# Decoding float64 weights in halves through PSUM between the products of a mixture of experts

## The chip, the cores and the metric

The kernel runs on one core of a Trainium2 chip. The metric is the device time of one execution in microseconds, the median over several runs. The core's engines are called as the profile calls them: PE (TensorE, matrix products; PEld are its weight loads), DVE (VectorE), ACT (ScalarE), POOL (GpSimd) and SP (SyncE, which issues DMAs).

## The reference

Three layers run one after the other on 3072 tokens. A chunked state-space attention gives rows of 256 numbers. A router sends each row to one of eight experts, each two products with a ReLU between. A dense layer of width 2048 follows, whose weights `w_in` and `w_out` arrive as float64.

```python
h = np.maximum(x[mask] @ w1[e], 0.0)          # eight experts, 256 -> 1024 -> 256
out[mask] = gate_w[mask, None] * (h @ w2[e])
...
h = x @ w_in                                  # 256 -> 2048, float64 weights
g = h * np.cos(h)
return (g @ w_out).astype(np.float32)         # 2048 -> 256
```

## The kernel before, in words

The program has three stages. The first (to about 136 us) computes attention and router and scatters each token's row into its expert's list in DRAM. The second (136 to 297 us) works through eight lists, `for e in range(E)`. The third (from 297 us) is the dense layer. The change lies in the second.

**A list.** List 0 has 256 places, lists 1 to 7 have 432. All products are made of pairs: a number is split into a high part of type fp32r and a remainder of the same type, and three matmuls stand for one. For each eighth f of the hidden width PE makes product f into a PSUM tile `ph` (L1235, six matmuls), ACT takes the ReLU's high part `hh` (L1239), DVE the remainder `hl` (L1240, reading `ph` and `hh`). From f = 3 on PE also makes the second product of f - 3 into `py` (L1203), which reads `hh` and `hl`; those of the last three eighths form the list's tail, after the f loop, for each of two halves m. ACT then copies `py` to `yd` (L1197). `ph` comes from the pool `psH` with four buffers, one PSUM bank each; `px` (the transposed rows of the next list, L1049) has two banks and `py` two.

**What goes beside it.** Between products the program's order on each engine is written out by hand: after each f, `side.take(k)` runs k steps of the decode (below), `next(gt[..])` steps of the gates of the next lists (small DVE instructions on `xg`, such as L840, L846, L863, and an exponential on ACT), and `ws.take()` one step of splitting the next list's weights: a copy `h` on ACT (L743) and a subtraction `l` on POOL (L752). After f = 5 PE transposes the next list's rows; ACT and DVE make `xh` and `xl` of them (L1055, L1057), the latter ahead of the last `hl` of the list.

**The decode.** The dense layer's weights come as float64, 16 pieces of 512 columns by 128 partitions, each 32-bit word of a number beside the other. `fetch(q)` loads piece q into one of two buffers `raw` (SP's queue). The generator `decode()` turns a piece into float32 in steps, one step to each `yield`: ACT scales the high words (`tb`, L1086); DVE shifts them (`ta`, L1088), merges the sign bit (L1090) and the top bits of the low word (L1094, or L1101 into `wof`). For the eight pieces of `w_in` ACT then makes the high part `ih` (L1096) and DVE the remainder `il` (L1098). `ta` and `tb` have one SBUF buffer each. Seven steps make a piece of `w_in`, five one of `w_out`, 96 in all. The generator is started at the end of list 0. The table `g.TE` says how many steps follow each product of each list, `g.SD` how many go into a list's tail: `SD[0]` once and `SD[1]` after each half, the latter not in list 7. In list 7 the split of the decoded output weights (`split_out`, L1114 on ACT and L1115 on POOL) goes beside the last decode steps.

**Loads.** All on SP's queue in the program's order: before list 0, the w2 of list 1 and the rows of list 2 (L883); in list 0, after f = 2 a fill of list 3's unused places (L870), after f = 4 the w1 of list 2 (L729) and, behind it, `fetch(0)` and `fetch(1)` (L1068); then the w2 of list 2 (L735) and the rows of list 3. Later pieces are fetched when the decode begins a piece, one ahead.

Of the kernel before, what the change touches and what calls it, by code (L numbers as in the profile page):

```python
# [8 lines left out]
F32 = mybir.dt.float32  # L9
# [11 lines left out]
NT, D, E, F, F2 = 3072, 256, 8, 1024, 2048  # L21
NSTEP = S // 128
SX = 4096
RW = 274
# [614 lines left out]
TWO_PI = 6.283185307179586  # L639
# [3 lines left out]
def tile_attention_moe_moe2(ctx: ExitStack, tc: tile.TileContext, A1, A2, X, BNh, BT, CT, cst_d, emb, tau, w1, w2, w_in, w_out, out):  # L643
    nc = tc.nc
    ET = mybir.EngineType
    g = G_()
# [19 lines left out]
    g.WARM = 12  # L666
    g.LD = "cnfz"
    g.HEAD = "k2 l0 i1 a0 z0 m0 c1 k2 z1 s1 k3 b0 p1 k6 i1 s2 e0 c2 k2 k1 i9 a1 b1 y0 e0 p2 e0 e0 t1 k6 t1 t1 t1 t1"
    g.SD = (1, 1)
    g.FIRST = 6  # L670
    g.GE = "vava"
    g.GW = "va"
# [8 lines left out]
    g.G1 = [(), (6, 3, 2, 2, 1, 0, 0, 0)] + [(3, 1, 2, 1, 1, 0, 0, 0)] * 6  # L681
    g.G2 = (0, 0, 0, 0, 2, 0, 2, 2)

    g.TE = [(0, 0, 0, 0, 0, 0, 0, 0)] + [(2, 1, 1, 1, 1, 1, 1, 1)] * 4 + [(2, 2, 2, 2, 2, 2, 1, 2)] + [(2, 2, 2, 2, 2, 2, 2, 2)] * 2
    g.L2 = "vvvv"
    g.WL = 16
    g.S1 = ("vvvv", "vpvp")
# [344 lines left out]
    with ExitStack() as mctx:  # L1032
        mp = mctx.enter_context(tc.tile_pool(name="mp", bufs=1, reuse_waits="tile"))
        mp2 = mctx.enter_context(tc.tile_pool(name="mp2", bufs=2, reuse_waits="tile"))
        wpool[1] = mctx.enter_context(tc.tile_pool(name="wB", bufs=1, reuse_waits="tile"))
        psX = mctx.enter_context(tc.tile_pool(name="psX", bufs=1, space=PSUM, reuse_waits="tile"))
        psH = mctx.enter_context(tc.tile_pool(name="psH", bufs=4, space=PSUM, reuse_waits="tile"))
        psO = mctx.enter_context(tc.tile_pool(name="psO", bufs=1, space=PSUM, reuse_waits="tile"))
        wof = mp.tile([128, 16 * D], F32, name="wof")

# [16 lines left out]
            nc.vector.tensor_tensor(out=xl, in0=px[:, :, :n], in1=xh.bitcast(F32), op=ALU.subtract)  # L1057
            yield xh, xl

        PL = 512  # L1060

        src = [w_in.bitcast(U32).rearrange("(k p) (q f) -> k q p f", p=128, f=2 * PL),
               w_out.bitcast(U32).rearrange("(q f p) d -> q p f d", p=128, f=2)]
# [1 line left out]
        def fetch(q):  # L1065
            raw = mp.tile([128, PL, 2], U32, tag="raw", name="raw", bufs=2)
            if q < 8:
                nc.sync.dma_start(raw.rearrange("p f w -> p (f w)"), src[0][q // 4, q % 4])  # L1068
            else:
                nc.sync.dma_start(raw.rearrange("p (f d) w -> p f (d w)", f=2), src[1][q - 8])  # L1070
            return raw

        def decode():

            ihf, ilf = ih.rearrange("p k f -> p (k f)"), il.rearrange("p k f -> p (k f)")
            V_ = nc.vector
            for q in range(16):
                raw = raw_.pop(0)
                if 1 <= q < 15:
                    raw_.append(fetch(q + 1))  # L1080
                L, H = raw[:, :, 0], raw[:, :, 1]
                ta = mp.tile([128, PL], U32, tag="ta", name="ta")
                tb = mp.tile([128, PL], U32, tag="tb", name="tb")
                yield

                nc.scalar.activation(tb.bitcast(F32), H.bitcast(F32), AF.Copy, scale=2.0 ** -112)  # L1086
                yield
                V_.tensor_scalar(ta, tb, 3, 0x7fffffff, op0=ALU.logical_shift_left, op1=ALU.bitwise_and)  # L1088
                yield
                V_.scalar_tensor_tensor(out=ta, in0=tb, scalar=0x80000000, in1=ta, op0=ALU.bitwise_and, op1=ALU.bitwise_or)  # L1090
                yield
                if q < 8:
                    s = slice(PL * q, PL * q + PL)
                    V_.scalar_tensor_tensor(out=ta, in0=L, scalar=29, in1=ta, op0=ALU.logical_shift_right, op1=ALU.bitwise_or)  # L1094
                    yield
                    nc.scalar.activation(ihf[:, s], ta.bitcast(F32), AF.Copy, scale=1.0 / TWO_PI)  # L1096
                    yield
                    V_.scalar_tensor_tensor(out=ilf[:, s], in0=ta.bitcast(F32), scalar=1.0 / TWO_PI, in1=ihf[:, s].bitcast(F32), op0=ALU.mult, op1=ALU.subtract)  # L1098
                else:
                    s = slice(PL * (q - 8), PL * (q - 8) + PL)  # L1100
                    V_.scalar_tensor_tensor(out=wof[:, s].bitcast(U32), in0=L, scalar=29, in1=ta, op0=ALU.logical_shift_right, op1=ALU.bitwise_or)  # L1101
                yield

        O = {}

# [16 lines left out]
        def overflow():  # L1122
            with tc.If(T > 0):
                with tc.For_i(0, T, 1) as i:
                    V_ = nc.vector
# [31 lines left out]
                    w2r = w2.rearrange("e f d -> (e f) d")  # L1157
                    nc.sync.dma_start(v1, w1r[bass.ds(r_1, D), :].rearrange("(k p) f -> p k f", p=128))
                    nc.sync.dma_start(v2, w2r[bass.ds(r_2, F), :].rearrange("(f p) d -> p f d", p=128))
                    vx = mp.tile([128, PL], F32, tag="ta", name="vx")[:, :RW]  # L1160
                    nc.sync.dma_start(vx, xs[bass.ds(r_3, 128), :])
                    ix = mp2.tile([128, 1], F32, tag="ix", name="ix")
                    nc.gpsimd.tensor_copy(ix, vx[:, 273:])
# [4 lines left out]
                        pass  # L1168
                    for m in range(2):
                        nc.tensor.transpose(px[:, m, :128], vx[:, 136 * m:136 * m + 128], ident)  # L1170
                    vt = mp.tile([128, PL], F32, tag="tb", name="vt")[:, :D].rearrange("p (m c) -> p m c", m=2)
                    nc.vector.tensor_copy(vt, px[:, :, :128])
                    py = [psO.tile([128, 512], F32, tag=f"py{m}", name="py") for m in range(2)]
                    vh = wof[:, :1024].rearrange("p (f c) -> p f c", f=8)
# [11 lines left out]
        load_w2(1)  # L1186
        xs_ = {1: xg, 2: rows_of(2)}
        numbers(1, xg, mp2, ET.Pool, nc.gpsimd)
        raw_ = []
        x_ = g.x0  # L1190
        gt = [steps["g"], None]

# [24 lines left out]
        for e in range(E):  # L1217
            w = {k: W[e][k].rearrange("p (a b) -> p a b", a=2 if k[1] == "1" else 8) for k in ("h1", "l1", "h2", "l2")}
            xh, xl = x_
            n = wide(e)  # L1220
            ws = Sides()
            if e + 1 < E:
                ws.add(split_w(e + 1))
            else:
                ws.add(split_out())
            py = [psO.tile([128, 512], F32, tag=f"py{m}", name="py") for m in range(2)]
            hs = {}
            for f in range(8):
# [12 lines left out]
                hs[f] = (hh, hl)
                if f >= 3:
                    q = f - 3
                    hh, hl = hs.pop(q)
                    for m in range(2):
                        second(py, m, q, w, hh, hl)
                side.take(g.TE[e][f])
                if f == 0 and 0 < e < E - 2:
                    xs_[e + 2] = rows_of(e + 2)
                if f == 2 and e + 3 < E:  # L1250
                    fill(e + 3)
                for _ in range((g.G1[e] if e else g.G0)[f] if e < E - 1 else 0):
                    next(gt[0])
                if f == 4 and e + 2 < E:
                    gt[1] = gates(xs_[e + 2], mp2, g.GE, e + 2)
                for _ in range((g.G2 if e else g.G20)[f] if e + 2 < E else 0):
                    next(gt[1])
                if f >= 1 or e == E - 1:
                    ws.take()
                if f == 4 and e + 2 < E:  # L1260
                    load_w1(e + 2)
                if (e, f) == (0, 4):
                    raw_ += [fetch(0), fetch(1)]
                if f == (g.PX if e else g.PX0) and e + 1 < E:
                    px = turn(e + 1, xs_.pop(e + 1))
                if f == (g.PX if e else g.PX0) + 1 and e + 1 < E:
                    tp = turned_parts(e + 1, px)
                    next(tp)
                if e == 0 and f == g.XL0:
                    nx = next(tp)  # L1270
            if e + 1 < E:
                x_ = nx
            ws.drain()
            if e + 2 < E:
                next(gt[1])
            gt[0] = gt[1]
# [182 lines left out]
```

## Time and profile before

| what | us |
|---|---|
| median of 3 runs (580.02 to 585.91) | 580.35 |
| the profiled execution, its own time | 577.3 |
| the profiled execution, span from first to last instruction | 575.6 |
| PE busy in the span | 547.3 |
| DVE busy | 443.9 |
| ACT busy | 298.1 |
| POOL busy | 308.9 |

The profile is of one execution. Its busy shares are averages over three unlike stages; what holds in the list stage is read from that stage's stretches. PE's matmuls overlap, so in a busy stretch the start of one matmul to the start of the next is the measure, not the duration of one.

### The profile page before, as it was taken

The numbers are of one execution on the slowest core, as the hardware profiler recorded it, in microseconds if no ns is written. First come the engines' busy times: TensorE is split into PE (matmuls) and PEld (weight loads), VectorE is DVE, ScalarE is ACT, GpSimd is POOL, SyncE is SP. The second block draws the span as 40 slices with busy tenths as digits, with TensorE's granted clock in tenths as the row PEclk, the third lists the DMA queues.
The fourth block names the chain that finished last, engine by engine and source line by source line (L and its number), as shares of the span: only waits on it lengthen the run. The fifth ranks groups of instructions, "written<-read, shape, count | busy, mean of one in ns | idle before, by whom it ended". The sixth has DMA issues, their size and how long they took to land.

```text
span 575.6 us, 11048 instructions
## 1 busy us (share of the span) xinstructions
PE 547.3 (95%) x4000; PEld 497.1 (86%) x4000; DVE 443.9 (77%) x878; ACT 298.1 (52%) x637; POOL 308.9 (54%) x343
## 2 busy tenths in 40 slices
PE   7798999998878999989999999999999999999994
PEld 5587887898868999989988999999999999999994
DVE  6999999866397898898859877766777777676882
ACT  6163543544375567667647546446445445445562
POOL 4323543462265485465636647647646745755763
PEclk9899999999999999999999999999999999999998
DMA  7899895137766556754210000000100100100000
GB/s 213 233 209 226 203 247 170 41 113 216 227 212 216 186 174 183 246 171 158 73 2 2 1 1 11 26 1 2 38 0 1 38 2 1 38 1 10 29 20 19
DMA packets 28993, 57.00 MB, mean 99 GB/s; under 512 B 7216, under 2 KB 16056, under 8 KB 28184
## 3 DMA queue, kind: packets, MB, share of 16 engines
q1 hardware_dynamic: 26184, 47.77, 29.3%
q0 software_dynamic: 2752, 8.51, 4.5%
q8 instruction: 32, 0.52, 0.4%
q14 instruction: 25, 0.20, 0.1%
HBM read 48.50 MB, written 11.07 MB: 103 GB/s over the span
## 4 chain that ended last, share of the span: by engine, by line
PE 56%; DVE 8%; issue 3%; ACT 2%; POOL 1%; POOLq 0%; ACTq 0%; DVEq 0%
PE po L1378 22%; PE pu L1344 22%; PE py L1203 6%; PE ph L1235 5%; DVE hl L1240 2%; DVE ta L1088 1%; POOL gl L1415 1%; DVE ta L1090 1%; DVE xl L1057 1%; DVE lg L840 1%; ACT hh L1239 1%; ACT h L743 1%; DVE ta L1094 1%; DVE xg L863 1%; PE spare L1344 0%
## 5 line engine op out<-in xcount | busy, mean ns | idle before, releaser
L1415 POOL TENSOR_TENSOR gl<-gg,gh 128x512 fp32r<-128x512 f32 (+1 forms) x111 | 125.8, 1139 | 105.0 <-PE pu L1344 59.7
L1405 ACT ACTIVATE cc<-ff,half 128x512 f32<-128x512 f32 (+1 forms) x112 | 74.3, 663 | 128.3 <-DVE ff L1403 128.2
L1401 DVE TENSOR_SCALAR tt<-pu 128x512 f32<-128x512 f32 (+1 forms) x110 | 67.4, 613 | 64.4 <-PE pu L1344 64.2
L1378 PE MATMUL po<-h,gl 128*128 128x256 f32 x384 | 108.2, 282 | 0.0
L1378 PE MATMUL po<-l,gh 128*128 128x256 f32 x384 | 108.2, 282 | 0.0
L1378 PE MATMUL po<-h,gh 128*128 128x256 f32 x382 | 107.6, 282 | 0.0
L752 POOL TENSOR_TENSOR l<-r,h 128x512 fp32r<-128x512 f32 x50 | 68.0, 1373 | 57.9 <-ACT h L743 57.4
L1378 PEld LDWEIGHTS po<-h,gh 128*128 128x128 f32 x382 | 72.3, 189 | 3.6
L1378 PEld LDWEIGHTS po<-l,gh 128*128 128x128 f32 x384 | 72.6, 189 | 3.1
L1378 PEld LDWEIGHTS po<-h,gl 128*128 128x128 f32 x384 | 73.0, 190 | 0.1
L1403 DVE SCALAR_TENSOR_TENSOR ff<-tt,pu 128x512 f32<-128x512 f32 (+1 forms) x110 | 67.0, 609 | 3.8
L1344 PE MATMUL pu<-yh,il 128*128 128x512 f32 (+1 forms) x192 | 68.5, 357 | 0.0
L1344 PE MATMUL pu<-yh,ih 128*128 128x512 f32 (+1 forms) x192 | 68.2, 355 | 0.0
L1344 PE MATMUL pu<-yl,ih 128*128 128x512 f32 (+1 forms) x192 | 68.0, 354 | 0.0
L1411 DVE SCALAR_TENSOR_TENSOR gg<-pu,cc 128x512 f32<-128x512 f32 (+1 forms) x110 | 66.6, 606 | 0.7 <-ACT cc L1405 0.4
L1414 ACT CAST gh<-gg 128x512 fp32r<-128x512 f32 (+1 forms) x112 | 60.8, 543 | 1.1 <-DVE tt L1401 0.5
L1240 DVE SCALAR_TENSOR_TENSOR hl<-ph,hh 128x432 fp32r<-128x432 f32 (+1 forms) x64 | 36.7, 576 | 22.5 <-ACT hh L1239 22.4
L1203 PE MATMUL py<-hl,h 128*128 128x432 f32 (+1 forms) x128 | 45.7, 357 | 4.7 <-DVE hl L1240 4.4
L1203 PE MATMUL py<-hh,h 128*128 128x432 f32 (+1 forms) x128 | 44.9, 351 | 1.9 <-ACT hh L1239 1.9
L1203 PE MATMUL py<-hh,l 128*128 128x432 f32 (+1 forms) x128 | 44.5, 348 | 0.0
L1239 ACT ACTIVATE hh<-ph 128x432 fp32r<-128x432 f32 (+1 forms) x64 | 32.8, 513 | 22.2 <-PE ph L1235 20.2
L1344 PEld LDWEIGHTS pu<-yl,ih 128*128 128x128 f32 x192 | 36.2, 188 | 5.6
(220 smaller groups left out, 1202.2 us busy)
## 6 DMA issues: line engine op xcount, KB each, us to landing
r<-in_w SPq DMA_DIRECT2D x32, 512.0 KB, 5.5
ac<-acd SPq DMA_DIRECT2D x10, 512.0 KB, 6.7
raw<-in_w_in SPq DMA_DIRECT2D x8, 512.0 KB, 4.5
raw<-in_w_out SPq DMA_DIRECT2D x8, 512.0 KB, 3.3
xg<-xs SPq DMA_DIRECT2D x7, 462.4 KB
xs<-zd SPq DMA_DIRECT2D x5, 462.4 KB
XB<-in_X SPq DMA_DIRECT2D x8, 256.0 KB
bt<-in_BT SPq DMA_DIRECT2D x6, 256.0 KB, 9.0
```

The source lines that it names most:

```text
L752: (nc.vector if engines[q] == "v" else nc.gpsimd).tensor_tensor(out=l[:, s], in0=W[e][rn][:, s], in1=h[:, s].bitcast(F32), op=ALU.subtract)
L1203: nc.tensor.matmul(py[m][:, :b_.shape[1]], lhsT=a_[:, q, 128 * m:128 * m + 128], rhs=b_, start=q == 0 and k == 0, stop=q == 7 and k == 2)
L1239: nc.scalar.activation(hh, ph[:, :n], AF.Relu)
L1240: nc.vector.scalar_tensor_tensor(out=hl, in0=ph[:, :n], scalar=0.0, in1=hh.bitcast(F32), op0=ALU.max, op1=ALU.subtract)
L1344: nc.tensor.matmul(PU[u], lhsT=a_[:, c, 128 * f:128 * f + 128], rhs=b_[:, c], start=c == 0 and k == 0, stop=c == 1 and k == 2)
L1378: nc.tensor.matmul(po[:, i], lhsT=a_[:, s], rhs=b_, start=first and per == 1, stop=q == NF - 1 and k == 2 and i == per - 1)
L1401: nc.vector.tensor_scalar(tt, pu, 0.25, MAGIC, op0=ALU.add, op1=ALU.add)
L1403: nc.vector.scalar_tensor_tensor(out=ff, in0=tt, scalar=-MAGIC, in1=pu, op0=ALU.add, op1=ALU.subtract)
L1405: nc.scalar.activation(cc, ff, AF.Sin, bias=half, scale=-TWO_PI)
L1411: nc.vector.scalar_tensor_tensor(out=gg, in0=pu, scalar=TWO_PI, in1=cc, op0=ALU.mult, op1=ALU.mult)
L1414: nc.scalar.copy(gh, gg)
L1415: (nc.vector if u >= len(units) else nc.gpsimd).tensor_tensor(out=gl, in0=gg, in1=gh.bitcast(F32), op=ALU.subtract)
```

## The change

The decode works in halves of 256 columns. Of each half, the scaled high words and the shifted word lie in one PSUM tile of the new pool `psD` (one bank, one buffer); only the word `tu` between the low-word merge and the sign merge lies in SBUF, with two buffers. The order of the two merges is exchanged. `psH` has three buffers in place of four. A half takes six steps for `w_in` and four for `w_out`, 160 in all, and the tables `g.TE` and `g.SD` are raised. The first two raw loads are issued before list 0, directly behind the rows of list 2, in place of after f = 4 of list 0. (In the overflow path two scratch tiles take the tag `tu`.)

```diff
-    g.SD = (1, 1)
+    g.SD = (2, 2)
...
-    g.TE = [(0, 0, 0, 0, 0, 0, 0, 0)] + [(2, 1, 1, 1, 1, 1, 1, 1)] * 4 + [(2, 2, 2, 2, 2, 2, 1, 2)] + [(2, 2, 2, 2, 2, 2, 2, 2)] * 2
+    g.TE = [(0, 0, 0, 0, 0, 0, 0, 0)] + [(3, 2, 2, 2, 2, 2, 2, 2)] * 4 + [(3, 3, 3, 3, 3, 3, 2, 2)] + [(3, 3, 3, 3, 3, 3, 3, 3)] * 2
...
-        psH = mctx.enter_context(tc.tile_pool(name="psH", bufs=4, space=PSUM, reuse_waits="tile"))
+        psH = mctx.enter_context(tc.tile_pool(name="psH", bufs=3, space=PSUM, reuse_waits="tile"))
+        psD = mctx.enter_context(tc.tile_pool(name="psD", bufs=1, space=PSUM, reuse_waits="tile"))
...
-        PL = 512
+        PL, PH = 512, 256
...
-                L, H = raw[:, :, 0], raw[:, :, 1]
-                ta = mp.tile([128, PL], U32, tag="ta", name="ta")
-                tb = mp.tile([128, PL], U32, tag="tb", name="tb")
-                yield
-
-                nc.scalar.activation(tb.bitcast(F32), H.bitcast(F32), AF.Copy, scale=2.0 ** -112)
-                yield
-                V_.tensor_scalar(ta, tb, 3, 0x7fffffff, op0=ALU.logical_shift_left, op1=ALU.bitwise_and)
-                yield
-                V_.scalar_tensor_tensor(out=ta, in0=tb, scalar=0x80000000, in1=ta, op0=ALU.bitwise_and, op1=ALU.bitwise_or)
-                yield
...
+                for h in range(0, PL, PH):
+                    L, H = raw[:, h:h + PH, 0], raw[:, h:h + PH, 1]
+                    tt = psD.tile([128, 2, PH], F32, tag="tb", name="tb")
+                    tb, ta = tt[:, 0], tt[:, 1]
+                    tu = mp.tile([128, RW], U32, tag="tu", name="tu", bufs=2)[:, :PH]
+
+                    nc.scalar.activation(tb, H.bitcast(F32), AF.Copy, scale=2.0 ** -112)
+                    tb, tv = tb.bitcast(U32), ta.bitcast(U32)
                     yield
+                    V_.tensor_scalar(tv, tb, 3, 0x7fffffff, op0=ALU.logical_shift_left, op1=ALU.bitwise_and)
                     yield
+                    V_.scalar_tensor_tensor(out=tu, in0=L, scalar=29, in1=tv, op0=ALU.logical_shift_right, op1=ALU.bitwise_or)
+                    yield
+                    s = slice(PL * (q % 8) + h, PL * (q % 8) + h + PH)
+                    if q < 8:
+                        V_.scalar_tensor_tensor(out=tv, in0=tb, scalar=0x80000000, in1=tu, op0=ALU.bitwise_and, op1=ALU.bitwise_or)
+                        yield
+                        nc.scalar.activation(ihf[:, s], ta, AF.Copy, scale=1.0 / TWO_PI)
+                        yield
+                        V_.scalar_tensor_tensor(out=ilf[:, s], in0=ta, scalar=1.0 / TWO_PI, in1=ihf[:, s].bitcast(F32), op0=ALU.mult, op1=ALU.subtract)
+                    else:
+                        V_.scalar_tensor_tensor(out=wof[:, s].bitcast(U32), in0=tb, scalar=0x80000000, in1=tu, op0=ALU.bitwise_and, op1=ALU.bitwise_or)
+                    yield
...
-        raw_ = []
+        raw_ = [fetch(0), fetch(1)]
...
-                if (e, f) == (0, 4):
-                    raw_ += [fetch(0), fetch(1)]
```

## Rows read from the trace of the kernel before

**Rows 1.** The page's first part, TensorE's line: busy time, share of the span, instructions.
```profile
PE 547.3 (95%) x4000; PEld 497.1 (86%) x4000; DVE 443.9 (77%) x878; ACT 298.1 (52%) x637; POOL 308.9 (54%) x343
```

**Rows 2.** Busy time of each engine in one stretch per list, lists 0 to 7 in order: from the start of the list's first product to that of the next list's. Columns: the stretch and its length, then busy time and instructions of PE, PEld, DVE, ACT and POOL, granted clock, DMA share, GB/s.
```profile
136.30:150.00 13.70, 13.01 (x105) 12.55 (x105) 9.42 (x25) 8.93 (x21) 4.51 (x6) 1.00 0.63 166
150.00:176.95 26.95, 21.10 (x106) 18.38 (x105) 19.16 (x33) 12.37 (x25) 13.07 (x13) 1.00 0.76 246
176.95:196.90 19.95, 19.83 (x106) 18.67 (x104) 15.44 (x23) 13.15 (x26) 11.93 (x10) 1.00 0.56 183
196.90:216.80 19.90, 19.87 (x106) 18.70 (x105) 17.67 (x30) 12.05 (x24) 11.93 (x11) 1.00 0.60 181
216.80:236.30 19.50, 19.50 (x106) 18.73 (x105) 17.38 (x27) 13.16 (x27) 12.48 (x10) 1.00 0.64 211
236.30:258.00 21.70, 20.06 (x105) 18.57 (x104) 20.09 (x32) 13.72 (x27) 11.84 (x10) 1.00 0.61 193
258.00:278.20 20.20, 19.85 (x106) 18.71 (x106) 17.98 (x27) 13.13 (x26) 10.93 (x8) 1.00 0.38 129
278.20:297.20 19.00, 19.00 (x98) 18.20 (x97) 12.85 (x17) 12.41 (x23) 11.91 (x8) 1.00 0.17 56
```

**Rows 3.** The timeline of TensorE in list 1: start, us, line, operation, and in brackets the idle time before it with what ended it.
```profile
159.10 0.47 PE L1203 MATMUL py<-hh,h 128*128 128x432 f32 x1 [1.92 <-ACT hh L1239]
...
165.91 0.59 PE L1049 MATMUL px<-ident,xg 108*128 108x108 f32 x4 [1.79 <-DVE xg L863]
...
174.70 0.46 PE L1203 MATMUL py<-hl,h 128*128 128x432 f32 x1 [1.49 <-DVE hl L1240]
```

**Rows 4.** The timeline of ScalarE at the start of list 1, same columns.
```profile
151.38 0.53 ACT L1239 ACTIVATE hh<-ph 128x432 fp32r<-128x432 f32 x1 [0.80 <-PE ph L1235]
157.97 0.66 ACT L1086 ACTIVATE tb<-raw 128x512 f32<-128x512 f32 x1 [6.06 <-DMA raw<-in_w_in]
...
159.06 0.62 ACT L743 CAST h<-r 128x512 fp32r<-128x512 f32 x1
```

**Rows 5.** The timeline of SyncE's issues around the start of list 1: list 2's rows, list 3's fill, list 2's w1, the first two raw loads.
```profile
142.07 0.37 SPq L883 DMA_DIRECT2D xg<-xs  x1
149.31 0.64 SPq L870 DMA_DIRECT2D xs<-zd  x1
150.07 0.97 SPq L729 DMA_DIRECT2D r<-in_w  x2
151.09 0.92 SPq L1068 DMA_DIRECT2D raw<-in_w_in  x2
```

**Rows 6.** Busy time by stretch around the start of list 1, columns as in the second group: DMA share and GB/s stand last.
```profile
142.00:148.00 6.00, 5.92 (x48) 5.49 (x46) 4.29 (x9) 4.36 (x10) 1.27 (x2) 1.00 0.76 204
148.00:150.00 2.00, 1.43 (x13) 1.41 (x12) 1.21 (x3) 1.07 (x3) 1.88 (x2) 1.00 0.02 2
```

**Rows 7.** VectorE's groups of instructions from 150 to 297.2 us (busy us, mean ns), then instructions by tile or line over the whole run (ns: minimum/median/maximum).
```profile
L1090 DVE SCALAR_TENSOR_TENSOR ta<-tb,ta 128x512 uint32<-128x512 uint32 x16 | 19.6, 1226 | 0.2
L1088 DVE TENSOR_SCALAR ta<-tb 128x512 uint32<-128x512 uint32 x16 | 12.1, 756 | 0.1
...
L1098 DVE SCALAR_TENSOR_TENSOR il<-ta,ih 128x512 fp32r<-128x512 f32 x8 | 9.4, 1181 | 0.2 <-ACT ih L1096 0.2
...
L1094 DVE SCALAR_TENSOR_TENSOR ta<-raw,ta 128x512 uint32<-128x512 uint32 x8 | 8.1, 1014 | 0.1
L1101 DVE SCALAR_TENSOR_TENSOR wof<-raw,ta 128x512 uint32<-128x512 uint32 x8 | 7.9, 986 | 0.1
...
L1088 DVE TENSOR_SCALAR ta<-tb x16: 410/427/3685, 159.6 to 287.1; 128x512 uint32<-128x512 uint32 x16
L1090 DVE SCALAR_TENSOR_TENSOR ta<-tb,ta x16: 682/1136/3624, 161.6 to 287.7; 128x512 uint32<-128x512 uint32 x16
...
L1240 DVE SCALAR_TENSOR_TENSOR hl<-ph,hh x64: 393/596/610, 137.9 to 293.1; 128x432 fp32r<-128x432 f32 x56, 128x256 fp32r<-128x256 f32 x8
```

**Rows 8.** The timelines of VectorE (DVE) and GpSimd (POOL) in lists 1 and 5.
```profile
166.29 4.37 DVE L840 TENSOR_TENSOR lg<-xg 108x32 f32<-108x32 f32 x1
...
166.83 3.79 POOL L752 TENSOR_TENSOR l<-r,h 128x512 fp32r<-128x512 f32 x3
...
248.38 3.69 DVE L1088 TENSOR_SCALAR ta<-tb 128x512 uint32<-128x512 uint32 x1
...
248.00 3.79 POOL L752 TENSOR_TENSOR l<-r,h 128x512 fp32r<-128x512 f32 x3
```

**Rows 9.** Groups of instructions: 256 elements wide, in list 0 (136.3 to 150 us), on VectorE and ScalarE, then ScalarE's tb from 150 to 297.2 us. Columns: busy us, mean ns, then the idle time before them and what ended it.
```profile
L1240 DVE SCALAR_TENSOR_TENSOR hl<-ph,hh 128x256 fp32r<-128x256 f32 x8 | 3.3, 416 | 1.7 <-ACT hh L1239 1.7
...
L1239 ACT ACTIVATE hh<-ph 128x256 fp32r<-128x256 f32 x8 | 3.1, 386 | 1.3 <-POOL few L836 1.3
...
L1086 ACT ACTIVATE tb<-raw 128x512 f32<-128x512 f32 x16 | 10.7, 667 | 9.8 <-DMA raw<-in_w_in 6.1 <-DVE ta L1090 2.6 <-DMA raw<-in_w_out 1.1
```

**Rows 10.** The timelines of VectorE and TensorE: in list 4 the hl of product 0 and the first matmul of product 3; in list 0 the hl of product 1 and the first matmul of product 4.
```profile
218.76 0.61 DVE L1240 SCALAR_TENSOR_TENSOR hl<-ph,hh 128x432 fp32r<-128x432 f32 x1 [1.20 <-ACT hh L1239]
...
220.30 0.36 PE L1235 MATMUL ph<-xh,h 128*128 128x432 f32 x1
...
139.67 0.39 DVE L1240 SCALAR_TENSOR_TENSOR hl<-ph,hh 128x256 fp32r<-128x256 f32 x1
...
140.08 0.28 PE L1235 MATMUL ph<-il,h 128*128 128x256 f32 x1
```

More of the change, by code (lines that the diff above doesn't have):

```diff
@@ L1090, in decode @@
-                V_.scalar_tensor_tensor(out=ta, in0=tb, scalar=0x80000000, in1=ta, op0=ALU.bitwise_and, op1=ALU.bitwise_or)
-                yield
-                if q < 8:
-                    s = slice(PL * q, PL * q + PL)
-                    V_.scalar_tensor_tensor(out=ta, in0=L, scalar=29, in1=ta, op0=ALU.logical_shift_right, op1=ALU.bitwise_or)
+                for h in range(0, PL, PH):
[5 more added lines that the diff above has]
+                    tb, tv = tb.bitcast(U32), ta.bitcast(U32)
@@ L1095, in decode @@
                     yield
-                    nc.scalar.activation(ihf[:, s], ta.bitcast(F32), AF.Copy, scale=1.0 / TWO_PI)
+                    V_.tensor_scalar(tv, tb, 3, 0x7fffffff, op0=ALU.logical_shift_left, op1=ALU.bitwise_and)
                     yield
[L1098 to L1101, printed above, removed]
@@ L1102, in decode @@
-                yield
+                    V_.scalar_tensor_tensor(out=tu, in0=L, scalar=29, in1=tv, op0=ALU.logical_shift_right, op1=ALU.bitwise_or)
[9 more added lines that the diff above has]
+                        V_.scalar_tensor_tensor(out=wof[:, s].bitcast(U32), in0=tb, scalar=0x80000000, in1=tu, op0=ALU.bitwise_and, op1=ALU.bitwise_or)
@@ L1159, in overflow @@
                     nc.sync.dma_start(v2, w2r[bass.ds(r_2, F), :].rearrange("(f p) d -> p f d", p=128))
-                    vx = mp.tile([128, PL], F32, tag="ta", name="vx")[:, :RW]
+                    vx = mp.tile([128, RW], F32, tag="tu", name="vx", bufs=2)
                     nc.sync.dma_start(vx, xs[bass.ds(r_3, 128), :])
@@ L1170, in overflow @@
                         nc.tensor.transpose(px[:, m, :128], vx[:, 136 * m:136 * m + 128], ident)
-                    vt = mp.tile([128, PL], F32, tag="tb", name="vt")[:, :D].rearrange("p (m c) -> p m c", m=2)
+                    vt = mp.tile([128, RW], F32, tag="tu", name="vt", bufs=2)[:, :D].rearrange("p (m c) -> p m c", m=2)
                     nc.vector.tensor_copy(vt, px[:, :, :128])
```

## The prediction

> **What bounds the kernel now.** The page's busy shares come first: PE holds 95% of the span [rows 1], so only a stretch in which PE stands still can give time back. The change touches the list stage alone, so the second view is busy time in one stretch per list, cut where PE starts a list's first product [rows 2]. The reader is to see one number: list 4 takes 19.50 us with PE busy for all of it, and list 7, which has no transposes for a next list, 19.00 us with PE busy for all of it. That is the floor. Over it stand list 1 with 7.45 us (26.95 - 19.50), list 2 with 0.45, list 3 with 0.40, list 5 with 2.20 and list 6 with 0.70: together 11.2 us. The granted clock is 1.00 in every row, so none of it is a slower PE. This 11.2 us is nearly all that the change can win.
>
> Third, PE's timeline says who ended the gaps of list 1 [rows 3]: 1.92 us until the ReLU part hh, 1.79 us until the gated rows xg, 1.49 us in the list's last products until hl. Fourth, ScalarE's timeline says why hh was late [rows 4]: its first decode instruction, tb, stood 6.06 us for the raw load and began at 157.97; the next hh, the gates' exponential and the split copies h queue behind it. Fifth, SyncE's issues [rows 5] and the DMA share [rows 6]: the two raw loads were issued at 151.09, behind list 3's fill and list 2's w1, while DMA moved 2 GB/s between 148 and 150.
>
> Last, why VectorE is late at list ends. The kind of instruction that reads and writes SBUF alone has a wide spread: the decode's shift takes 410 ns at best, 427 in the median and 3685 at worst; its sign merge 682, 1136 and 3624; hl, which reads PSUM and one SBUF tile, 393 to 610 over all 64 [rows 7]. The long ones coincide with GpSimd: an add of 108x32 elements takes 4.37 us from 166.29 and ends as GpSimd's run of three products l ends (166.83 + 3.79); the shift at 248.38 takes 3.69 us beside the run that began at 248.00 [rows 8]. That one precedes the 2.20 us of list 5.
>
> **The change part by part.** The sum is made against the profiled execution (577.3 us, span 575.6) and carried over to the median of 580.35 as a difference.
>
> *Raw loads.* Two 512 KB loads leave SyncE's queue at 151.09, behind a fill and a w1, and enter it directly behind list 2's rows at 142.07, some 0.4 us later; no instruction waits ahead of them there, and the buffers are new. Queued in front of the fill (149.31) and w1 (150.07), they use the stretch 148 to 150 that moves nothing [rows 5, 6]. They carry 1.05 MB; at the 204 GB/s of 142 to 148 that is 5.1 us if they had the queue alone, so part of them runs past 150 and w1 may come up to about 1 us later. The second decode load keeps its place. List 1's 7.45 us divide by the three named gaps: (1.92 + 1.79)/5.20 = 0.71, so 5.3 us hang on the raw wait and 2.1 us on the tail. What is late next is the split copy h behind its w1 load: it was first executed at 159.06, hidden by the raw wait, and will now wait itself. Bounds: 0 to 5.3 us; I take 4.7, near the top, because the loads finish long before the first use at about 152.
>
> *PSUM and halves on VectorE.* Before: 16 shifts, 16 merges, 24 low-word merges and 8 residuals, 57.1 us busy (12.1 + 19.6 + 8.1 + 7.9 + 9.4) [rows 7]. After: 16 x 2 x 3 + 8 x 2 = 112 instructions of 256 elements, each with a PSUM operand and at most one SBUF input. The nearest row is hl of list 0, 128x256 from PSUM and SBUF, 416 ns [rows 9]: 46.6 us, 10.5 us less. At best speed the old ones would cost 16 x 0.41 + 40 x 0.68 = 33.8 us [rows 7], with the low-word merge and the residual taken at the sign merge's best, so by instruction cost alone the edit adds 12.8 us; it pays only through the 23.3 us of blocking that it takes away. Lower bound: 10.5 us less; upper: blocking stays, 46.6 + 23.3 = 69.9, 12.8 more. I take the lower, because no PSUM-reading hl among 64 exceeded 610 ns.
> The Trainium skill, "SBUF — State Buffer", section "Who interferes with whom", says that a VectorE instruction with at most one SBUF input and outside the two-port modes does not contend with GpSimd; the trace agrees, by the 610 ns maximum of hl against 3685 of the shift. A rule that speaks against the change is in "Perfetto Trace Analysis", section "Optimizing Scalar/DVE Operations" (the Trainium skill): VectorE's fixed access cost is about 125 ns on PSUM against 60 on SBUF; by that alone 112 instructions would carry an estimated 7.3 us more. The 416 ns of the row contain it already.
>
> What VectorE's relief is worth on the path: list 5's 2.2 us follow from a blocked shift, so 1.6 comes back and 0.6 stays. List 1's tail of 2.1 us follows from a blocked add of the gates, which stays in SBUF; but GpSimd's run of three l was long because ScalarE released its copies in a bunch after the raw wait. 1.6 comes back. The 1.55 us of lists 2, 3 and 6 I leave: the gates' instructions and the xl, xh pair ahead of the last hl are unchanged, and two steps per product in place of one take the same 0.8 us.
>
> *ScalarE.* 32 tb and 16 ih at 386 ns [rows 9] in place of 16 at 667 and 8 like them: 0.77 against 0.67 a pair, 24 x 0.10 = 2.4 us over seven lists, in which it is busy for 12 to 14 of 20 us [rows 2]. Hidden.
>
> *One PSUM bank for the decode.* tb and the shifted word share one buffer, so each half's tb waits for the last VectorE instruction of the half before, and ScalarE's hh and h stand behind it. Today tb has waited so for 2.6 us in all [rows 9]. Two handoffs a half (tb to shift, ih to residual), each about 0.39 us of ScalarE: 0.8 us a half, most of it beside hl or gates. Bounds: 0 to 3.8 halves x 0.8 = 3.0 us a list; I take 0.2 us a list, 1.3 us over lists 1 to 6, as the steps of a half spread over three products, 7.3 us.
>
> *Three banks for the first products.* Product f+3 now waits for hl of f. In list 4 hl of the first product ended at 219.37 and product 3 began at 220.30: 0.93 us to spare [rows 10]. In list 0, with shorter products, hl ended at 140.06 and product 4 began at 140.08: nothing to spare. 0.2 us for list 0; bounds 0 to about 1 us a list, if an SBUF-only gate instruction is held between the first two hl.
>
> *Numbers of steps.* The decode has 96 steps before and 160 after (6 or 4 a half); the raised counts give 23 a list in lists 1 to 4, 28, 30 and 26 of which it needs 10 in list 7. It ends a product or two sooner than now, so the split of the output weights does not wait.
>
> Sum: 4.7 + 1.6 + 1.6 - 1.3 - 0.2 = 6.4 us. Profiled execution 570.9, **median 573.9 us**. The stage after is PE's own chain, so a gain here stays.
>
> **The rivals.**
> (a) *Only the loads count.* The blocking moves to what stays in SBUF: the gates' adds and scalings, which GpSimd held as long (4.37 us) as any decode step [rows 8]. For it: that row. Against it: the decode has most of VectorE's long instructions. Gain 4.7 + 0.3 - 1.5 = 3.5 us: 576.9.
> (b) *The raw loads delay w1.* They run in front of list 3's fill and list 2's w1; 1.05 MB at 204 GB/s pushes w1 by up to 3 us and ScalarE stands at h where it stood at tb. Against it: the empty stretch at 148 to 150. Half of the 5.3 us stays: 6.4 - 2.1 = 4.3 us gained, 576.1.
> (c) *Slower: the handoffs set VectorE's pace.* Place: lists 1 to 5, which have decode and gates. VectorE's busy time is 15.4 to 20.1 us a list [rows 2], on average 17.9; less 1.5 for the relief, plus 3.0 of exposed handoffs, is 19.4, and the floor is 19.5. From there each further microsecond lengthens the list, as ScalarE, standing at tb, also holds hh. Should all 3.0 us come out: 5 x 3.0 - 4.7 = 10.3 us slower, 590.7. For it: list 5 already runs at 20.09 of 21.70. Against it: handoffs fall beside hl in two of three products.
>
> **How the numbers follow.** Forecast 0.53, (a) 0.22, (b) 0.13, (c) 0.12. Forecast's own range: 569.5 (all 11.2 us, less 0.3) to 576. With (a) and (b) up to 577 and half of (c)'s price, 582 leaves out the worst of (c): range 569.5 to 582. One per cent, about what a measurement of this kernel tells from no change, is 5.8 us: faster means below 574.5. Most of the forecast lies there, little of (a) and (b): 0.50. Slower (above 586.2) is (c) nearly in full: 0.09. Within: 0.41.
>
> **What would show it.** Right: raw issued within 2 us of list 2's rows, tb of list 1 without a DMA wait and beginning before 153; list 1 at 20 to 20.5 us, list 5 at 20 to 20.3; decode instructions on VectorE at 0.40 to 0.45 us with no maximum above 0.7; PE never waiting over 0.3 us at a first product for hl. Wrong: ScalarE idle for w1 past 157; tb waits on VectorE above 1 us many times; lists 2 to 6 longer than now.

## The result, and the profile after

The changed kernel takes 585.62 us (median of 22 runs, 581.70 to 588.71) against 581.18 for the kernel before beside it: ratio 1.0063, 95% interval 1.0043 to 1.0083. A gain of 6.4 us was forecast; it is 3.7 to 4.4 us slower, outside the range.

Busy time of the changed kernel in one stretch per list, cut and laid out as in [rows 2] (last columns: granted clock, DMA share, GB/s):

```profile
142.20:156.20 14.00, 13.29 (x104) 12.61 (x105) 9.41 (x25) 8.83 (x21) 4.77 (x7) 1.00 0.85 235
156.20:179.60 23.40, 21.56 (x106) 20.15 (x105) 14.89 (x41) 12.97 (x29) 12.05 (x13) 0.93 0.72 220
179.60:199.20 19.60, 19.60 (x106) 18.71 (x106) 15.12 (x34) 13.17 (x29) 12.18 (x11) 1.00 0.69 194
199.20:223.65 24.45, 22.08 (x105) 20.26 (x104) 16.34 (x36) 13.61 (x31) 11.36 (x10) 0.89 0.61 192
223.65:243.95 20.30, 20.30 (x105) 19.44 (x104) 15.62 (x35) 12.85 (x29) 11.40 (x10) 0.96 0.59 190
243.95:267.10 23.15, 20.22 (x105) 18.70 (x105) 17.74 (x41) 13.38 (x30) 11.40 (x10) 1.00 0.54 180
267.10:289.60 22.50, 20.56 (x106) 18.74 (x105) 15.78 (x38) 13.51 (x30) 10.24 (x8) 1.00 0.38 121
289.60:308.60 19.00, 19.00 (x98) 18.22 (x97) 9.51 (x20) 12.49 (x25) 10.23 (x8) 1.00 0.07 25
```

List 1 fell from 26.95 to 23.40 us. But list 3 rose from 19.90 to 24.45, list 4 from 19.50 to 20.30, list 5 from 21.70 to 23.15 and list 6 from 20.20 to 22.50, and in lists 1, 3 and 4 the granted clock is no longer 1.00. The stage is 166.2 us from the first product of list 0 to the dense layer's first, against 160.7. VectorE is less busy in every list from 1 on: 114.4 us in the eight rows against 130.0. So the engine that was to be relieved is relieved. TensorE gains nothing by it: the 6 us that ScalarE stood for the first raw load are gone, but TensorE stands still for 9.8 us in the eight rows (166.4 less 156.6 busy) against 8.7 before (160.9 less 152.2), at other places, and is busy for 156.6 us against 152.2, as three rows lie in part at the lower clock.

The parts that went as forecast first. SyncE's issues and ScalarE's first tb, to be held against [rows 4] and [rows 5]:

```profile
148.64 0.37 SPq L883 DMA_DIRECT2D xg<-xs  x1
149.06 0.83 SPq L1069 DMA_DIRECT2D raw<-in_w_in  x2
...
157.58 0.53 ACT L1242 ACTIVATE hh<-ph 128x432 fp32r<-128x432 f32 x1 [0.80 <-PE ph L1238]
158.01 0.40 ACT L1089 ACTIVATE tb<-raw 128x256 f32<-128x256 f32 x1
```

The raw loads leave 0.4 us behind list 2's rows and tb begins with no wait, 0.4 us after the list's first hh. VectorE's decode by groups (busy us, mean ns), to be held against [rows 7]:

```profile
L1092 DVE TENSOR_SCALAR tb<-tb 128x256 uint32<-128x256 uint32 x32 | 13.6, 426 | 6.2 <-ACT tb L1089 6.2
L1094 DVE SCALAR_TENSOR_TENSOR tu<-raw,tb 128x256 uint32<-128x256 uint32 x32 | 13.3, 417 | 0.7
...
L1098 DVE SCALAR_TENSOR_TENSOR tb<-tb,tu 128x256 uint32<-128x256 uint32 x16 | 6.8, 427 | 0.3
L1104 DVE SCALAR_TENSOR_TENSOR wof<-tb,tu 128x256 uint32<-128x256 uint32 x16 | 6.7, 421 | 0.4
L1102 DVE SCALAR_TENSOR_TENSOR il<-tb,ih 128x256 fp32r<-128x256 f32 x16 | 6.7, 417 | 1.4 <-ACT ih L1100 1.4
```

That is 112 instructions and 47.1 us (forecast 46.6; before 57.1), none above 433 ns.

Now what went wrong: list 3, just ahead of its tail and in it. First ScalarE, then VectorE, then TensorE (in brackets the idle time and what ended it):

```profile
213.84 0.39 ACT L1100 ACTIVATE ih<-tb 128x256 fp32r<-128x256 f32 x1 [2.90 <-DVE tb L1098]
214.12 0.61 ACT L743 CAST h<-r 128x512 fp32r<-128x512 f32 x1
214.63 0.53 ACT L1242 ACTIVATE hh<-ph 128x432 fp32r<-128x432 f32 x1
216.16 0.40 ACT L1089 ACTIVATE tb<-raw 128x256 f32<-128x256 f32 x1 [1.00 <-DVE il L1102]
216.50 0.60 ACT L743 CAST h<-r 128x512 fp32r<-128x512 f32 x1
217.00 0.88 ACT L1056 CAST xh<-px 128x864 fp32r<-128x864 f32 x1
217.78 0.54 ACT L1242 ACTIVATE hh<-ph 128x432 fp32r<-128x432 f32 x1
```

```profile
210.95 1.99 DVE L840 TENSOR_TENSOR lg<-xg 108x32 f32<-108x32 f32 x1
...
213.39 0.42 DVE L1098 SCALAR_TENSOR_TENSOR tb<-tb,tu 128x256 uint32<-128x256 uint32 x1
215.19 0.61 DVE L1243 SCALAR_TENSOR_TENSOR hl<-ph,hh 128x432 fp32r<-128x432 f32 x1 [1.39 <-ACT hh L1242]
215.72 0.41 DVE L1102 SCALAR_TENSOR_TENSOR il<-tb,ih 128x256 fp32r<-128x256 f32 x1
```

```profile
218.36 0.64 PE L1206 MATMUL py<-hh,h 128*128 128x432 f32 x1 [1.84 <-ACT hh L1242]
219.54 0.73 PE L1206 MATMUL py<-hl,h 128*128 128x432 f32 x1 [0.54 <-DVE hl L1243]
220.06 0.56 PE L1206 MATMUL py<-hh,l 128*128 128x432 f32 x1
220.42 0.56 PE L1206 MATMUL py<-hh,h 128*128 128x432 f32 x1
```

To be read from the top: ih stands 2.90 us for VectorE's merge (L1098). The merge itself is late because a gates' add (L840) held VectorE for 1.99 us, where its median is 0.18; it ended with GpSimd's run beside it, at 212.9. Behind ih in ScalarE's order come a copy h and hh; the matmuls that hh reads were done at 211.8, and it begins at 214.63. VectorE in turn waits 1.39 us for that hh, does hl and the residual il, and only when il is done may tb overwrite the shared buffer: ScalarE stands 1.00 us more. Behind tb come the copy h, xh and the hh of the last product, at 217.78, 3.6 us after its product was done. TensorE waits 1.84 us for it. Summed over the list stage (who waited for whom: us, times, longest):

```profile
ACT ih L1100 <- DVE tb L1098: 19.4, 12, 2.9
ACT tb L1089 <- DVE wof L1104: 16.3, 13, 1.9
...
ACT tb L1089 <- DVE il L1102: 7.6, 9, 1.0
```

That is 43.3 us of ScalarE's time behind decode results, where the kernel before had 9.5, the 2.6 at tb of [rows 9] and the 6.9 at ih of this line:

```profile
ACT ih L1096 <- DVE ta L1094: 6.9, 6, 2.7
```

### The profile page after: what moved, and what is told of

The parts are those of the page before. It is cut to its first block, busy times and chain, and to the rows that moved or that the text cites. A ratio compares the mean times of both kernels' runs of the same rounds, so it can differ in the third digit from the quotient of the medians.

```text
span 587.1 us, 11143 instructions
## 1 busy us (share of the span) xinstructions
PE 555.0 (95%) x4000; PEld 503.9 (86%) x4000; DVE 428.5 (73%) x934; ACT 299.0 (51%) x661; POOL 304.0 (52%) x343
## 4 chain that ended last, share of the span: by engine, by line
PE 56%; DVE 8%; ACT 4%; issue 3%; POOL 1%; POOLq 0%; ACTq 0%
PE po L1379 22%; PE pu L1345 21%; PE py L1206 6%; PE ph L1238 5%; DVE hl L1243 2%; ACT hh L1242 1%; POOL gl L1416 1%; ACT h L743 1%; DVE tu L1094 1%; DVE wof L1104 1%; DVE tb L1092 1%; DVE xl L1058 1%; DVE lg L840 1%; ACT xg L865 1%; PE spare L1345 0%
## 5 line engine op out<-in xcount | busy, mean ns | idle before, releaser
L752 POOL TENSOR_TENSOR l<-r,h 128x512 fp32r<-128x512 f32 x50 | 64.5, 1303 | 64.4 <-ACT h L743 64.3
L1206 PE MATMUL py<-hh,h 128*128 128x432 f32 (+1 forms) x128 | 46.3, 362 | 2.5 <-ACT hh L1242 2.5
L1206 PE MATMUL py<-hh,l 128*128 128x432 f32 (+1 forms) x128 | 45.8, 358 | 0.0
L1238 PE MATMUL ph<-xh,h 128*128 128x432 f32 x112 | 41.3, 369 | 0.0
L788 POOL DMA_INDIRECT xs<-yr,pi x24 | 26.9, 1121 | 27.5 <-ACT yr L260 10.3
```

The lines of the kernel that those rows point to most:

```text
L752: (nc.vector if engines[q] == "v" else nc.gpsimd).tensor_tensor(out=l[:, s], in0=W[e][rn][:, s], in1=h[:, s].bitcast(F32), op=ALU.subtract)
L1206: nc.tensor.matmul(py[m][:, :b_.shape[1]], lhsT=a_[:, q, 128 * m:128 * m + 128], rhs=b_, start=q == 0 and k == 0, stop=q == 7 and k == 2)
```

## The experiments

Each kernel was run beside the kernel before on one chip. The list durations below are worked out from the traces (start of a list's first product to that of the next), the waits are ScalarE's, at tb and ih, for VectorE. Ratios compare medians, while a row's durations are of one execution, so that the two can differ by some microseconds.

| kernel | ratio (95%) | lists 0 to 7, us | stage | waits |
|---|---|---|---|---|
| before | 1 | 13.66 26.95 19.95 19.88 19.52 21.73 20.15 18.85 | 160.7 | 9.5 |
| changed | 1.0063 (1.0043-1.0083) | 13.98 23.41 19.57 24.48 20.31 23.17 22.47 18.81 | 166.2 | 43.3 |
| changed, again | 1.0082 (1.0049-1.0116) | 13.74 23.37 19.58 24.47 20.32 23.17 22.46 18.79 | 165.9 | 43.4 |
| loads alone | 0.9921 (0.9894-0.9947) | 13.87 23.30 19.93 19.88 19.52 23.29 20.15 18.85 | 158.8 | 9.7 |
| loads, three banks | 0.9938 (0.9919-0.9958) | 13.89 20.82 20.03 19.85 19.52 21.72 20.12 18.82 | 154.8 | 11.1 |
| changed, loads back | 1.0171 (1.0106-1.0235) | 14.05 28.43 24.52 24.41 20.18 23.14 22.50 18.79 | 176.0 | 48.1 |
| changed, tb in SBUF | 0.9922 (0.9894-0.9950) | 13.99 21.57 19.66 20.36 19.89 20.89 19.53 18.81 | 154.7 | 23.8 |
| changed, ih on VectorE | 1.0114 (1.0085-1.0142) | 12.38 24.25 20.20 25.17 19.53 22.86 22.49 18.81 | 165.7 | 43.1 |
| both edits | 0.9961 (0.9929-0.9992) | 14.20 25.62 19.55 19.56 19.55 19.56 19.55 18.81 | 156.4 | 0 |
| both, gates' words in PSUM | 0.9924 (0.9890-0.9958) | 13.71 19.83 19.53 19.56 21.60 22.09 19.55 18.81 | 154.7 | 1.0 |
| full width | 0.9883 (0.9843-0.9923) | 13.84 20.73 19.53 19.58 19.52 19.58 19.52 18.82 | 151.1 | 2.9 |

### The loads alone

```diff
-        raw_ = []
+        raw_ = [fetch(0), fetch(1)]
...
-                if (e, f) == (0, 4):
-                    raw_ += [fetch(0), fetch(1)]
```

> The kernel before with the two raw loads alone moved behind list 2's rows; decode, banks and steps unchanged. Theory A (the changed kernel loses because ScalarE, in order, stands behind VectorE's decode results in the one PSUM buffer, 43 us against 9.5, and hh stands behind it): the loads alone win what the prediction took for them, 4 to 5 us, so 576 to 577.5, ratio 0.992 to 0.994, list 1 at 21 to 22 us. Theory B (the third bank missing from the first products makes the loss): the same. Theory C (the loss lies ahead of the lists or in the clock, whatever the decode does): no gain, 580 to 585.

574.26 us against 578.83, 4.6 us less. By the medians the prediction's 4.7 us for this term holds. The one profiled execution shows less, a stage of 158.8 us for 160.7: list 5 runs partly at half the clock (granted 0.50 from 252 to 255 us; 23.29 us), and list 1, expected at 21 to 22, takes 23.30, with 1.00 us still standing at the transposes and 2.00 at its tail.

### The bank

```diff
-        psH = mctx.enter_context(tc.tile_pool(name="psH", bufs=4, ...))
+        psH = mctx.enter_context(tc.tile_pool(name="psH", bufs=3, ...))
```

> The kernel before with the loads moved and three buffers for the first products in place of four; decode unchanged, the freed bank unused. Theory A: within 1 us of the run with the loads alone, as hl ended ahead of the third product after it in nearly all rows. Theory B: 4 to 8 us above it, 581 to 585, with PE waiting at first products for hl. Theory C: as the loads alone.

574.50 us, the interval overlaps that of the loads alone, and list 0 takes 13.89 us against 13.87. The missing fourth bank costs nothing that shows beside the old decode. In the changed kernel's profile too TensorE waits for hl at no first product, so theory B falls.

### The loads back at their old place

> The changed kernel with the two raw loads back at their old place (after product 4 of list 0). If the loads and the decode's new form add up: 4 to 5 us above the changed kernel, ratio 1.012 to 1.018, ScalarE's first tb standing some 6 us for the load again and list 1 at 26 to 27 us. If the wait of tb for the half before hides what the loads give: ratio 1.005 to 1.009, as the changed kernel.

Ratio 1.0171, list 1 at 28.4 us, and ScalarE's first tb stands for the load again:

```profile
162.66 0.40 ACT L1089 ACTIVATE tb<-raw 128x256 f32<-128x256 f32 x1 [5.91 <-DMA raw<-in_w_in]
```

List 1 was expected at 26 to 27 us, and list 2 lengthened as well (24.5): TensorE stood 4.82 us in list 1 at a first product for hl, a wait that hangs on the number of banks. So the loads' gain is in the changed kernel in full, 5 to 6 us by the ratios (1.0171 against 1.0082 and 1.0063), and what the new decode loses is about 8 to 9 us (1.0063 against 0.9921).

### The changed kernel again

> The changed kernel once more, beside the others on one chip. Theory A: ratio 1.003 to 1.009, ScalarE's waits for decode results at 40 to 45 us again, stalls of TensorE at hh and at the transposes in lists 3, 5 and 6 again, but list 0 beginning at 136 to 137 us as in the other kernels (its 142.2 came from falls of the clock in the stage before, that come and go). Theory C (the stage before the lists is slower in the changed kernel): list 0 begins at 141 to 143 us again.

The lists agree with the first profile within 0.3 us each, stalls and clock falls included; they belong to the kernel. List 0 began at 140.3 us here, not at 136 to 137: that part of the expectation missed. The three kernels run together with this one began it at 139.1 to 139.7, full width among them, and the four of the first group, tb in SBUF among them, at 135.6 to 136.6 (the run with the loads back, made later, at 140.8); so the start does not go by the decode, and theory C falls. The medians leave little room for a slower first stage, as the list stage alone is 5.2 to 5.5 us longer and the median 3.7 to 4.8.

### tb in SBUF

```diff
-                    tt = psD.tile([128, 2, PH], F32, tag="tb", name="tb")
-                    tb, ta = tt[:, 0], tt[:, 1]
-                    tu = mp.tile([128, RW], U32, tag="tu", name="tu", bufs=2)[:, :PH]
+                    ta = psD.tile([128, PH], F32, tag="tb", name="ta")
+                    tb = mp.tile([128, RW], U32, tag="tu", name="tb", bufs=2)[:, :PH]
...
-    V_.scalar_tensor_tensor(out=tu, in0=L, scalar=29, in1=tv, ...)
+    V_.scalar_tensor_tensor(out=tv, in0=tb, scalar=0x80000000, in1=tv, ...)
...
-    V_.scalar_tensor_tensor(out=tv, in0=tb, scalar=0x80000000, in1=tu, ...)
+    V_.scalar_tensor_tensor(out=tv, in0=L, scalar=29, in1=tv, ...)
```

> The changed kernel with tb in two SBUF buffers and only the shifted word in PSUM (the sign merge goes back ahead of the low merge, so that every VectorE instruction still has at most one SBUF input). tb no longer waits for VectorE; ih still does. Theory A: ScalarE's wait for VectorE falls from 43 to about 20 us and half of the loss beside the loads' gain comes back: 580 to 582, ratio 0.998 to 1.002. Theory B and theory C: as the changed kernel, ratio 1.004 to 1.008.

574.28 us against 578.83: better than expected. Not half, but all of the loss is gone, with ih still waiting 21.1 us (the other 2.7 us of the table are one wait of tb, in list 5). The same place as above, ScalarE in list 3:

```profile
204.77 0.38 ACT L1099 ACTIVATE ih<-ta 128x256 fp32r<-128x256 f32 x1 [2.80 <-DVE ta L1097]
205.05 0.61 ACT L743 CAST h<-r 128x512 fp32r<-128x512 f32 x1
205.56 0.53 ACT L1241 ACTIVATE hh<-ph 128x432 fp32r<-128x432 f32 x1
205.99 0.44 ACT L1089 ACTIVATE tb<-raw 128x256 f32<-128x256 f32 x1
206.32 0.61 ACT L743 CAST h<-r 128x512 fp32r<-128x512 f32 x1
206.82 0.89 ACT L1056 CAST xh<-px 128x864 fp32r<-128x864 f32 x1
207.60 0.55 ACT L1241 ACTIVATE hh<-ph 128x432 fp32r<-128x432 f32 x1
```

ih stands 2.80 us, as there; but tb does not wait here, and the last hh comes right behind xh. The edit moves tb out of PSUM, gives it two buffers and changes the order of the merges back; a second PSUM bank for the decode, with the order kept, was not tried, so it is the wait that is shown to cost, not PSUM.

### ih on VectorE, and both edits

```diff
-    nc.scalar.activation(ihf[:, s], ta, AF.Copy, scale=1.0 / TWO_PI)
+    V_.tensor_scalar(ihf[:, s], ta, 1.0 / TWO_PI, None, op0=ALU.mult)
```

> The changed kernel with ih made by VectorE; tb stays in the one PSUM buffer. With the changed kernel (both waits), the run with tb in two SBUF buffers (only the wait for ih) and the run without either wait this fills the square. Theory A1 (the wait of tb for the half before is what loses, the wait for ih is harmless): tb still waits 20 to 25 us for VectorE, 583 to 586, ratio 1.002 to 1.008. Theory A2 (either wait alone is harmless, only both together overrun the product's time of 2.4 us): 574 to 578, ratio 0.992 to 0.998.

> The same as the run with tb in two SBUF buffers, and ih is made by VectorE in place of ScalarE (16 instructions of 256 elements, about 0.42 us each, 6.7 us of VectorE more): ScalarE never waits for the decode. Theory A: hh is on time, lists 2 to 6 at 19.5 to 20.3 us, 574 to 577, ratio 0.987 to 0.993, and fewer stretches at half the clock in the list stage. Theory B: as the changed kernel, ratio 1.004 to 1.008. Theory C: as the changed kernel.

With ih on VectorE and tb still in the one PSUM buffer: 587.41 against 581.71, ratio 1.0114. The wait did not go, it moved into tb:

```profile
ACT tb L1089 <- DVE il L1102: 26.8, 14, 4.2
```

With the 16.3 us behind wof, as before, tb waits 43.1 us, where 20 to 25 were expected, and the ratio lies above the expected 1.002 to 1.008. This settles A1 against A2: the wait of tb for the half before loses alone, the wait for ih alone does not. The square is 1.0063 with both waits, 1.0114 with tb's, 0.9922 with ih's, 0.9961 with neither. It does not tell which wait from how much of it, as tb's alone is 43.1 us and ih's 21.1. Nor is ih's wait free: lists 2 to 6 take 100.3 us with it and 97.8 with neither.

With neither, lists 2 to 6 stand at 19.55 us each, as expected, but list 1 takes 25.6 and the ratio misses the expected 0.987 to 0.993. VectorE, GpSimd and TensorE at the tail of list 1:

```profile
165.70 5.06 DVE L844 TENSOR_TENSOR lg<-lg,mx 108x32 f32<-108x32 f32 x1
...
164.45 6.27 POOL L752 TENSOR_TENSOR l<-r,h 128x512 fp32r<-128x512 f32 x5
...
172.30 0.46 PE L1205 MATMUL py<-hl,h 128*128 128x432 f32 x1 [3.87 <-DVE hl L1242]
```

One subtraction of the gates on 108x32 elements, with two inputs in SBUF, lasted 5.06 us and ended with GpSimd's fifth product l in a row; TensorE stood 3.87 us for the hl behind it.

### The gates' words in PSUM

```diff
+        g.gp = psD.tile([128, 512], F32, name="gp")
...
-        V_.tensor_tensor(out=lg, in0=xg[:, :, 128:136], in1=xg[:, :, 264:272], op=ALU.add)
+        V_.tensor_copy(lg, xg[:, :, 128:136])
+        V_.tensor_tensor(out=lg, in0=lg, in1=xg[:, :, 264:272], op=ALU.add)
...
-        V_.tensor_scalar_add(r, r, 1e-6)
+        V_.tensor_scalar_add(ra, r, 1e-6)
```
(on the kernel with both edits; for these lists lg and ra are slices of g.gp)

> The run without either wait (tb in SBUF, ih on VectorE), and the gates' small words lg, r and gs in the free part of the decode's PSUM bank, so that their VectorE instructions are no longer held by GpSimd (one held 5.06 us in list 1 there, the list's whole stall; one copy of 108x32 more per list). Theory A: lists 1 to 6 all below 20.3 us, list stage 150 to 152 us, 570 to 573, ratio 0.983 to 0.989. If the held gate instruction was not the cause: list 1 stays at 24 to 26 us, ratio 0.993 to 0.998.

List 1 is at 19.83 us, so the held instruction was its cause; but lists 4 and 5 rise to 21.6 and 22.1, and the ratio, 0.9924, is short of the expectation. What is held now is the scaling of xg, the one step left that reads and writes SBUF alone (VectorE and GpSimd in list 4):

```profile
220.93 3.66 DVE L875 TENSOR_SCALAR xg<-xg,gs 108x256 f32<-108x256 f32 x1
...
221.95 2.48 POOL L753 TENSOR_TENSOR l<-r,h 128x512 fp32r<-128x512 f32 x2
```

### Full width

```diff
-                ta = mp.tile([128, PL], U32, tag="ta", name="ta")
-                tb = mp.tile([128, PL], U32, tag="tb", name="tb")
+                ta = psD.tile([128, PL], F32, tag="ta", name="ta").bitcast(U32)
+                tb = mp.tile([128, PL], U32, tag="tb", name="tb", bufs=2)
```
(on the kernel before, with the loads moved and three buffers in `psH`; 96 steps and the tables as before)

> The kernel before with the loads moved and the decode in full width: tb in two SBUF buffers, the shifted word of 512 columns alone in the decode's PSUM bank, three buffers for the first products; steps, order and tables as before. No VectorE instruction of the decode has two SBUF inputs or SBUF alone. VectorE's decode: 56 instructions of 0.69 us, 38.6 us against 57.1 in the kernel before and 47.2 in halves; 24 handoffs, as before. Theory A: lists 2 to 6 at 19.5 to 20.0 us with ScalarE's waits below 12 us: 571 to 574.5, ratio 0.985 to 0.992. If halves are what helps (shorter instructions between two hl): no better than the loads alone, 0.992 to 0.995.

573.59 us against 581.71, ratio 0.9883: it is faster than the kernel before and the changed one. Lists 2 to 7 stand at the floor, with TensorE busy throughout. Lists 1, 3 and 5 of the same view as above, two of VectorE's decode lines (ns: minimum/median/maximum), and ScalarE's largest wait for the decode:

```profile
152.95:173.65 20.70, 19.79 (x106) 18.65 (x105) 15.83 (x32) 12.69 (x25) 12.77 (x13) 1.00 0.81 235
...
193.20:212.80 19.60, 19.60 (x106) 18.78 (x105) 16.75 (x28) 12.57 (x25) 11.41 (x10) 1.00 0.60 183
...
232.30:251.90 19.60, 19.60 (x106) 18.78 (x105) 16.47 (x30) 13.67 (x27) 11.36 (x10) 1.00 0.66 212
...
L1089 DVE TENSOR_SCALAR ta<-tb x16: 677/684/695, 157.0 to 280.2; 128x512 uint32<-128x512 uint32 x16
L1091 DVE SCALAR_TENSOR_TENSOR ta<-tb,ta x16: 678/687/697, 159.8 to 281.0; 128x512 uint32<-128x512 uint32 x16
...
ACT ih L1097 <- DVE ta L1095: 2.9, 4, 0.9
```

The reader is to see 19.60 of 19.60 in the second and third row, no decode instruction above 697 ns, and 2.9 us of waits where the changed kernel has 43.3. Against the same kernel without the decode's PSUM (loads, three banks) the stage is 3.7 us shorter; by ratios, 0.9883 against 0.9938, the intervals touch. The run also gives tb a second buffer, and ScalarE's waits fall from 11.1 us to 2.9; what the second buffer and what the PSUM word brought was not told apart.

## Why the prediction was wrong, step by step

*The raw loads* were right: 4.7 us forecast, 4.6 measured alone, and 5 to 6 inside the changed kernel. The wait for w1 that was named as next in line came in the run with the loads alone (the copy h of list 1 stood 1.62 and 1.64 us), not in the changed kernel, where no copy of list 1 stood for a load; rival (b) did not happen.

*VectorE's price* was right: 47.1 us for 46.6. The Trainium skill, "SBUF — State Buffer", section "Who interferes with whom", says which forms contend with GpSimd, those with two SBUF inputs or in a two-port mode; the runs agree: a subtraction held for 5.06 us was held no longer with one input in PSUM, and a scaling from SBUF to SBUF was, for 3.66.

*What the relief is worth* was wrong in part. 3.2 us were counted on lists 1 and 5. In halves it gave nothing on the whole (154.7 us with tb in SBUF, 154.8 with the old decode, the loads and three banks): list 5 won 0.8 us (20.89 for 21.72), list 1 lost as much (21.57 for 20.82). At full width it was 3.7, the second buffer of tb included.

*The banks*: 0.2 us forecast, nothing seen.

*The step that failed* is "One PSUM bank for the decode", 0.2 us a list, put at 1.3 us in all (six times 0.2 is 1.2). Between the changed kernel and the run with tb in SBUF lie 11.4 us of list stage in single executions (166.1 against 154.7), 8 to 9 us by the ratios. The mechanism was named there in so many words: tb waits for the half before and hh stands behind it. Its size was held against 2.6 us of waits in a kernel where four steps lie between tb's last reader and the next tb for `w_in`, and two for `w_out`. In the changed kernel the last reader of the shared buffer is the step just ahead, and tb waits in 22 of 32 halves, 15 times for 1 us or more; the prediction had named such waits as a sign of being wrong. The price was counted as ScalarE's own 0.39 us a handoff "beside hl or gates".

List 6 shows the price most plainly: no ih is left there, and the granted clock is 1.00 in both kernels. First the changed kernel's waits in it, then the list with tb in SBUF, to be held against 22.50 above:

```profile
ACT tb L1089 <- DVE wof L1104: 9.5, 8, 1.5
...
252.95:272.50 19.55, 19.55 (x106) 18.77 (x105) 16.34 (x39) 13.15 (x29) 10.31 (x8) 1.00 0.43 142
```

That is 2.9 us in one list, where 0.2 were forecast. What counts is that hh, and by it TensorE, stands behind tb. In list 3 hh began 0.1, 0.9, 0.7, 2.7, 2.7, 1.7, 2.8 and 3.6 us after the matmuls of its product, product by product; with tb in SBUF 0.1, 0.1, 0.0, 1.8, 0.7, 0.1, 1.1 and 0.8. In lists 2 and 4 of the changed kernel it is back at 0.1 us ahead of the tail, so a late hh can be made up for. In list 3 a late merge and then a waiting tb fall close to the tail, and nothing is left to make them up.

Which lists lengthen, the rows suggest: ScalarE's busy time and its waits for the decode make 20.5, 24.0, 21.6 and 23.0 us in lists 1, 3, 5 and 6 of the changed kernel, over the floor of 19.5, and 16.9 and 14.4 in lists 2 and 4, the one at the floor, the other longer by its clock alone. With tb in SBUF no list is above 19.6. This was not tried by itself.

*Rival (c)* had the handoffs and the held hh, but the wrong engine as the bound: it added them to VectorE's busy time. VectorE fell to 114.4 us busy and waited more for ScalarE (31.0 us at hl, 22.4 before); the order of ScalarE's queue was the bound. Rival (a) has a part: the gates' add held for 1.99 us in list 3, and holds of 5.06 and 3.66 us, with TensorE standing behind them, in the two runs with next to none of ScalarE's waits.

*The clock* had no term in the sum. Lists 1, 3 and 4 ran at a granted 0.93, 0.89 and 0.96, in both profiles of the changed kernel, and the run with tb in SBUF at 1.00; so by an estimate from these rows 23.4 x 0.07 + 24.45 x 0.11 + 20.3 x 0.04 = 5.1 us of the 11.4 passed as lost clock. The rest is TensorE standing still, 9.8 us against 3.9. Against the kernel before, the lower clock is the larger part of the stage's 5.5 us: TensorE stands 1.1 us longer and is busy 4.4 us longer. Both falls came within 2 us after a stall; that the stalls brought them is not shown.

## What to carry to other kernels

A scratch buffer that two in-order engines fill and empty in turn can cost more than its handoffs: whoever refills it stands for the other's last read, with everything queued behind it. Before giving work its own PSUM bank, look at which word needs PSUM at all; here one operand there was enough, and the word that ScalarE refills stayed in SBUF with two buffers. And price a moved wait by what stands behind it in its engine's order, list by list, not by the engine's own time for the handoff.

## What the runs showed of the hardware that was not expected

A VectorE instruction that GpSimd holds can be held for longer than one GpSimd instruction: for 4.37 us to the end of a run of three products in [rows 8], for 5.06 us to the end of a run of five in the run with both edits. It is not always so: in the full-width run a gates' add (L840) began at 183.31 beside two products that GpSimd made from 183.25 to 185.79, and was done after 1.28 us, with the first of them. What decides stays open.

The decode's shift, 512 columns, takes 410 ns at best and 427 in the median from SBUF to SBUF, but up to 3685 when it is held [rows 7]; from SBUF to PSUM it takes 677 to 695. So the hold is what makes the slower form the cheaper one here.

In list 3 TensorE's granted clock fell just after the stall of 1.84 us, which ended at 218.36: it is 1.00 from 218.0 to 218.4 and 0.50 from 218.6 to 221, and the stall of 0.54 us came after the fall. Matmuls then began 0.36 us apart in place of 0.20, at the lower of the two clock levels, 1.2 GHz for 2.4. In the kernel before, list 1 had stalls of 1.92 and 1.79 us [rows 3] at a granted 1.00 throughout [rows 2], and list 5 of the changed kernel stalls of 1.46 and 1.44 us, also at 1.00; what makes the difference stays open.
